# Five unread filler products taken out of a decode block's tail, and half of one row of small products cut narrower

## The chip, the core and the metric

The kernel runs on one core of one Trainium2 chip. TensorE (PE in the profile, its weight loads PEld), VectorE (DVE), ScalarE (ACT), GpSimd (POOL) and SyncE (SP, which issues most of the DMAs) each run their own list of instructions and wait for each other by semaphores. The metric is the time of one execution on the device in microseconds. TensorE's clock is granted by a throttle: the profile shows the granted share, 1.0 or 0.5.

## The reference

One decode step of a transformer block with conditioning, for two sequences (B = 2, one token each, D = 512), all in float32:

```python
mod = (silu(c) @ w_mod).reshape(2, 6, 1, 512)      # sa, ca, ga, sb, cb, gb
h = layernorm(x) * (1 + ca) + sa
x = x + ga * attention(h)                          # 32 query heads, 8 key heads of 128,
                                                   # last 4096 positions of the cache, then @ wo
h = layernorm(x) * (1 + cb) + sb
x = x + gb * (silu(h @ w1) @ w2)                   # w1: 512 x 1792, w2: 1792 x 512
```

The inputs that are read come to 97.5 MB, nearly all of it cache and weights, each read once.

## The kernel before

All weights and caches stream through a ring of eight slots in SBUF (`slots`), loaded by SP in the order of use: w_mod, wq, then keys and values in four groups each, wo, w1, w2. A load waits until the products that read its slots before are done.

TensorE's work is in program order (`inorder`). Products with a wide weight matrix keep two activation columns as the stationary operand in a 128x32 piece of the array, and stream 512 columns of weights past it; four such calls, one for each 32 columns of the array (g = 0 to 3), run side by side. In float32 a call stands as two products in the trace.

The tail of the kernel, to which the change belongs, is a chain:

1. `busy(4)` (L414): four filler products. `busy(n)` (L384) issues n products of `id4` with a zero tile `warm` of 512 columns into the PSUM bank `junk` (L382), which nobody reads.
2. wo: 32 calls into `acc_o` (L417).
3. `gather` (L396): ACT copies acc_o to SBUF in two halves (L400), and four calls of 128 columns add up the four pieces into `ao` (L404).
4. DVE turns ao, adds the residual to x1T and sums it (L433 to L444); TensorE forms the mean (L446), DVE the centred, scaled activations hT_b and the squares (L449 to L454).
5. w1: 16 calls of 448 columns into `hid` (L459), with the variance `var_b` between its halves (L468). ACT takes the root (L470).
6. DVE turns hid, scales it, and forms the SiLU with an exponential on ACT (L475 to L487); the result is uT.
7. w2: rows 0 to 10 as calls of 512 columns into `acc_yw` (L491). ACT copies that to `y_sb` in two halves (L513).
8. The last three rows of w2 are used the other way round, "turned" (L503): pieces of the weights are the stationary operand, 128x32 or, in the first of these rows, 128x64, and two columns of uT stream past. Between them the same form adds up y_sb. All go into `yx`.
9. DVE adds the residual (L524), and ACT issues the store (L525).

Five more fillers stand in the tail: one in `gather` behind ACT's copies (`fill=1`), one behind ao, one behind the mean and two behind w1's products.

The loads of w2 come in five pieces, rows 0 to 7, 8 to 10, 11, 12 and 13. The last four wait for slots that wo's products leave.

Of the kernel before, what the change touches and what calls it, by code (L numbers as in the profile page):

```python
# [23 lines left out]
def adaln_block(  # L24
# [34 lines left out]
    def const(shape, name):  # L59
        return consts.tile(shape, F32, name=name)  # L60

    def bank(tag, name):
        return (psum1 if tag in "CO" else psum).tile([P, 512], F32, tag=tag, name=name)
# [155 lines left out]
    hT, uT = const([P, 4, 32], "hT_b"), const([P, F // P, 32], "uT")  # L219
# [9 lines left out]
    for n in range(2):  # L229
        q_ps = bank("D", f"q{n}")  # L230
        for k in range(4):
            for g in range(4):
# [5 lines left out]
                    start=(k == 0),  # L238
                    stop=(k == 3),
# [3 lines left out]
        for g in range(G):  # L243
# [4 lines left out]
                start=True,  # L248
                stop=True,
# [134 lines left out]
    def busy(n):  # L384

        for _ in range(n):
            inorder(nc.tensor.matmul(  # L387
                junk[0:32, :],
                id4,
                warm,  # L390
                start=True,
                stop=True,
            ))


    def gather(acc, wide, name, start, stop, fill=0):  # L396

        sb_ = once.tile([P, D], F32, tag="wide", name=name)
        for c in (slice(0, D // 2), slice(D // 2, D)):
            inorder(nc.scalar.copy(sb_[:, c], wide[:, c]))  # L400
        if fill:
            busy(fill)
        for g in range(4):
            inorder(nc.tensor.matmul(  # L404
                acc[32 * g : 32 * g + 32, :],
                id4,
                sb_[:, g * P : (g + 1) * P],
                start=start,
                stop=stop,
            ))  # L410

    acc = bank("D", "acc_o")
    ao = bank("A", "ao")[:, :P]
    busy(4)  # L414
    for q in range(32):
# [5 lines left out]
            start=(q < 4),  # L421
            stop=(q >= 28),
        ))
    gather(ao, acc, "acc_o_sb", True, True, fill=1)
    busy(1)
    T2, WIDE = F // P, 11
    w2t = {}
    for lo, hi in ((0, 8), (8, 11), (11, 12), (12, 13), (13, T2)):
# [15 lines left out]
    nc.vector.tensor_reduce(ks, x1T.rearrange("p k b -> p b k"), axis=AX.X, op=ALU.add)  # L444
    mean = bank("B", "mean_b")
    inorder(nc.tensor.matmul(mean[:, :B], mean512, ks, start=True, stop=True))  # L446
    busy(1)
    dT = once.tile([P, 4, B], F32, tag="dT", name="dT")
    nc.vector.tensor_sub(dT, x1T, mean[:, None, :B].to_broadcast([P, 4, B]))  # L449
    nc.vector.tensor_mul(hT[:, :, 0:32:16], dT, cbT[:, :, 0:32:16])  # L450
# [6 lines left out]
    for k in range(4):  # L457
        for g in range(4):
# [4 lines left out]
                start=(k == 0),  # L463
                stop=(k == 3),
            ))
        if k == 1:
# [3 lines left out]
            nc.scalar.activation(std, var[:, :B], AF.Sqrt, bias=eps_t)  # L470
            rstd = once.tile([P, B], F32, tag="rstdb", name="rstd_b")
            nc.vector.reciprocal(rstd, std)
    busy(2)
    hidT = once.tile([P, T2, 32], F32, tag="pr", name="hidT")
    nc.vector.transpose(hidT, hp.rearrange("p (m t) -> p t m", t=T2))  # L475
    z = once.tile([P, T2, B], F32, tag="z", name="z")
# [12 lines left out]
    for tt in range(WIDE):  # L489
# [5 lines left out]
            start=(tt < 4),  # L495
            stop=(tt >= WIDE - 4),
        ))

    def turned_products(rows, u, ks=range(4), start=False, stop=False, m=32):

        for k in ks:
            for g in range(0, P, m):
                inorder(nc.tensor.matmul(  # L503
                    yT[g : g + m, k, :, 0],
                    rows[:, k * P + g : k * P + g + m],
                    u,
                    start=start and k == 0,
                    stop=stop and k == 3,
                ))
# [2 lines left out]
    for c in (slice(0, D // 2), slice(D // 2, D)):  # L512
        inorder(nc.scalar.copy(y_sb[:, c], yw[:, c]))  # L513
    for h, tt in enumerate(range(WIDE, T2)):
        turned_products(
            w2t[tt],
            uT[:, tt, 0:32:16],
            start=(h == 0),
            stop=(tt == T2 - 1),
            m=32 if h else 64,  # L520
        )
        if h < 2:
            turned_products(y_sb, id4[:, 0:32:16], range(2 * h, 2 * h + 2))
    inorder(nc.vector.tensor_tensor_scan(yo, g0, yx, 0.0, op0=ALU.mult, op1=ALU.add))  # L524
# [48 lines left out]
```

## Time and profile before

| | us |
|---|---|
| median of 3 runs | 233.94 (233.76 to 233.95) |
| the profiled execution | 233.89 |
| its span, first to last instruction | 232.3 |
| PE busy in the span | 125.5 (54%) |
| DVE, ACT, POOL busy | 21.9, 17.3, 5.2 |
| data moved | 97.66 MB, mean 420 GB/s |

The mean granted clock of TensorE over the span is 0.801. Times within the trace count from the start of the span. A row of the timeline or of a group gives the engine, the line of the kernel, the operation, `output<-inputs` by the program's names, shapes and a count; an arrow in brackets names what ended the idle time before it. `slots<-in_B_w_dram` stands for a load of w1 or w2. A stretch's row gives its length, the busy time and number of instructions of the engine asked for, the granted clock, the DMA share and the GB/s.

### The profile page before, as it was taken

What the parts mean: (1) busy time and instruction counts of PE and PEld (TensorE: products, weight loads), DVE (VectorE), ACT (ScalarE), POOL (GpSimd) and SP (SyncE); (2) the same over time, 40 slices, a digit from 0 to 9 for tenths busy, and PEclk for the clock granted to TensorE, in tenths of its full rate; (3) what the DMA queues carried; (4) which work ended last, traced back from release to release, by engine and by line L of the source; (5) the groups of instructions that cost most, each with busy time, mean ns of one, the idle gap of its engine ahead of it and who ended that gap; (6) DMA issues with size and microseconds to landing.
All of it is one profiled execution on the core that took longest, in us unless ns stands there. A gap on an engine that the chain in (4) does not pass through costs nothing.

```text
span 232.3 us, 2204 instructions
## 1 busy us (share of the span) xinstructions
PE 125.5 (54%) x976; PEld 42.4 (18%) x976; DVE 21.9 (9%) x74; ACT 17.3 (7%) x39; POOL 5.2 (2%) x22
## 2 busy tenths in 40 slices
PE   0004905840950781495096068139509506999877
PEld 0001401320210221121033012112202102232223
DVE  0005330110021000003000001200000210000230
ACT  2000210000012010001001000100100100000331
POOL 4003010000000000000000000000000000000000
PEclk9999995985796596578579659957857965999999
DMA  7999898998989989899899999999999999999993
GB/s 271 432 495 429 372 530 361 508 398 361 530 372 508 395 364 519 384 496 398 374 496 406 496 395 386 474 418 474 406 395 465 429 446 406 432 392 444 414 410 133
DMA packets 2916, 97.66 MB, mean 420 GB/s; under 512 B 460, under 2 KB 476, under 8 KB 1116
## 3 DMA queue, kind: packets, MB, share of 16 engines
q1 hardware_dynamic: 2748, 97.52, 97.6%
q8 instruction: 7, 0.11, 0.2%
q10 hardware_dynamic: 160, 0.01, 0.0%
q14 instruction: 1, 0.01, 0.0%
HBM read 97.53 MB, written 0.01 MB: 420 GB/s over the span
## 4 chain that ended last, share of the span: by engine, by line
DMA 76%; PE 22%; issue 1%; DVE 1%; SPq 0%
DMA slots<-in_A_v_cache_dram 50%; PE o L323 16%; DMA slots<-in_A_wq_dram 15%; DMA slots<-in_B_w_dram 10%; PE q L234 4%; PE acc_yw L491 1%; PE yx L503 1%; PE qT L244 0%; DVE q_sb L242 0%; SPq L102 0%; DVE xc L93 0%; DVE yo L524 0%
## 5 line engine op out<-in xcount | busy, mean ns | idle before, releaser
L272 PE MATMUL s<-slots,qs 128*32 128x512 f32 x256 | 36.6, 736 | 32.6 <-DMA slots<-in_A_k_cache_dram 32.6
L323 PE MATMUL o<-slots,probs 128*32 128x512 f32 x256 | 37.0, 739 | 25.5 <-DMA slots<-in_A_v_cache_dram 25.5
L323 PEld LDWEIGHTS o<-slots,probs 128*32 128x32 f32 x256 | 11.6, 129 | 47.7 <-issue 47.7
L272 PEld LDWEIGHTS s<-slots,qs 128*32 128x32 f32 x256 | 9.2, 132 | 56.7 <-issue 31.4
L197 PE MATMUL m_a<-slots,scT 128*32 128x256 f32 x32 | 4.0, 447 | 20.4 <-DVE scT L189 20.4
L234 PE MATMUL q<-slots,hq_T 128*32 128x512 f32 x64 | 8.9, 703 | 8.4 <-DMA slots<-in_A_wq_dram 8.4
L284 DVE TENSOR_REDUCE mx<-s 128x1 f32<-128x512 f32 x4 | 2.8, 692 | 68.1 <-PE s L272 68.1
L387 PE MATMUL junk<-warm,id 128*32 128x512 f32 x18 | 8.6, 595 | 0.3 <-DVE oTn L347 0.3
L336 ACT ACTIVATE ob<-o,rl 128x256 f32<-128x256 f32 x8 | 3.4, 470 | 64.7 <-PE o L323 64.7
L347 DVE COPY oTn<-oT 128x16 f32<-128x16 f32 x4 | 0.7, 185 | 67.9 <-PE oT L339 67.9
L417 PE MATMUL acc_o<-slots,oTn 128*32 128x512 f32 x64 | 7.1, 593 | 0.0
L200 PE MATMUL m_sp<-slots,scT 128*32 128x512 f32 x32 | 6.6, 712 | 0.0
L298 ACT COPY bias<-bp 128x1 f32<-128x1 f32 x4 | 0.6, 159 | 79.4 <-PE bp L294 79.4
L339 PE MATMUL oT<-id,ob 128*128 128x4 f32 x32 | 4.2, 255 | 2.3 <-ACT ob L336 2.3
L197 PEld LDWEIGHTS m_a<-slots,scT 128*32 128x32 f32 x32 | 1.1, 117 | 21.2 <-DVE scT L189 20.4
L339 PEld LDWEIGHTS oT<-id,ob 128*128 128x128 f32 x32 | 3.9, 191 | 5.9 <-ACT ob L336 5.9
L234 PEld LDWEIGHTS q<-slots,hq_T 128*32 128x32 f32 x64 | 2.3, 126 | 14.1 <-issue 14.1
L305 PE MATMUL lp<-rowsum,same 128*128 128x1 f32 x8 | 1.7, 282 | 5.6 <-ACT pr L300 3.2
L491 PE MATMUL acc_yw<-slots,uT 128*32 128x512 f32 x22 | 2.8, 599 | 1.6 <-DMA slots<-in_B_w_dram 1.6
L459 PE MATMUL hid<-slots,hT_b 128*32 128x448 f32 x32 | 3.4, 544 | 0.5 <-DMA slots<-in_B_w_dram 0.5
L303 DVE STREAM_TRANSPOSE probs<-pr 128x512 f32<-128x512 f32 x4 | 2.8, 711 | 7.2 <-ACT pr L300 7.2
L286 PE MATMUL mT<-ident,mx 128*1 128x128 f32 x8 | 1.5, 271 | 3.3 <-DVE mx L284 3.3
(108 smaller groups left out, 60.1 us busy)
## 6 DMA issues: line engine op xcount, KB each, us to landing
slots<-in_w_mod_dram SPq DMA_DIRECT2D x1, 6144.0 KB, 17.2
slots<-in_A_wo_dram SPq DMA_DIRECT2D x1, 6144.0 KB, 26.1
slots<-in_B_w_dram SPq DMA_DIRECT2D x1, 2688.0 KB
slots<-in_A_wo_dram SPq DMA_DIRECT2D x1, 2048.0 KB, 30.1
slots<-in_B_w_dram SPq DMA_DIRECT2D x1, 2048.0 KB
slots<-in_B_w_dram SPq DMA_DIRECT2D x1, 896.0 KB
slots<-in_B_w_dram SPq DMA_DIRECT2D x1, 768.0 KB
slots<-in_B_w_dram SPq DMA_DIRECT2D x3, 256.0 KB, 16.1
```

Of the source, the lines that this page charges most:

```text
L197: nc.tensor.matmul(m_a[r, :], scT[:, k, :], ab[:, g], start=(k == 0), stop=(k == 3))
L200: nc.tensor.matmul(m_sp[r, :], scT[:, k, :], cd[:, g], start=(k == 0), stop=(k == 3))
L234: inorder(nc.tensor.matmul(q_ps[32 * g : 32 * g + 32, :], hq_T[:, k, :], wqt[:, k, lo : lo + 4 * DH], start=(k == 0), stop=(k == 3),))
L272: inorder(nc.tensor.matmul(s_ps[32 * c : 32 * c + 32, :], stat(grp, v, s), kt[grp][:, lo : lo + 512], start=(s == 0 and v == 0), stop=(s = ...
L284: nc.vector.tensor_reduce(mx, s_ps, axis=AX.X, op=ALU.max)
L323: inorder(nc.tensor.matmul(o_ps[r : r + 32, :], probs[grp % 2][:, 32 * n + 16 * s : 32 * n + 16 * s + 32], vt[grp][:, lo : lo + 512], star ...
L336: nc.scalar.activation(o_sb[:, c], o_ps[:, c], AF.Copy, scale=rl)
L339: inorder(nc.tensor.matmul(cols[:, 4 * v : 4 * v + 4], o_sb[:, v * DH : (v + 1) * DH], id4[:, 4 * v : 4 * v + 4], start=True, stop=True,))
L387: inorder(nc.tensor.matmul(junk[0:32, :], id4, warm, start=True, stop=True,))
L417: inorder(nc.tensor.matmul(acc[32 * g : 32 * g + 32, :], oTn[:, q, :], wot[q], start=(q < 4), stop=(q >= 28),))
L459: inorder(nc.tensor.matmul(hp[32 * g : 32 * g + 32, :], hT[:, k, :], w1t[k][:, g * FC : (g + 1) * FC], start=(k == 0), stop=(k == 3),))
L491: inorder(nc.tensor.matmul(yw[32 * g : 32 * g + 32, :], uT[:, tt, :], w2t[tt], start=(tt < 4), stop=(tt >= WIDE - 4),))
```

## The change

Five calls of `busy` go: the one in `gather` with its parameter, and those behind ao, behind the mean and the two behind w1. The four ahead of wo's products stay. The first turned row of w2 (row 11) was eight calls of 128x64; now its first two groups of 128 outputs are eight calls of 128x32, and the other two are four of 128x64. What is added up is the same.

```diff
-    def gather(acc, wide, name, start, stop, fill=0):
+    def gather(acc, wide, name, start, stop):
 
         sb_ = once.tile([P, D], F32, tag="wide", name=name)
         for c in (slice(0, D // 2), slice(D // 2, D)):
             inorder(nc.scalar.copy(sb_[:, c], wide[:, c]))
-        if fill:
-            busy(fill)
         for g in range(4):
...
-    gather(ao, acc, "acc_o_sb", True, True, fill=1)
-    busy(1)
+    gather(ao, acc, "acc_o_sb", True, True)
...
     inorder(nc.tensor.matmul(mean[:, :B], mean512, ks, start=True, stop=True))
-    busy(1)
...
             nc.vector.reciprocal(rstd, std)
-    busy(2)
     hidT = once.tile([P, T2, 32], F32, tag="pr", name="hidT")
...
     for h, tt in enumerate(range(WIDE, T2)):
-        turned_products(
-            w2t[tt],
-            uT[:, tt, 0:32:16],
-            start=(h == 0),
-            stop=(tt == T2 - 1),
-            m=32 if h else 64,
-        )
+        for half in range(2):
+            turned_products(
+                w2t[tt],
+                uT[:, tt, 0:32:16],
+                range(2 * half, 2 * half + 2),
+                start=(h == 0),
+                stop=(tt == T2 - 1),
+                m=32 if h or half == 0 else 64,
+            )
```

TensorE's list from wo's products to w2's, before (a number behind a name is a buffer's):

```order
L417 MATMUL acc_o<-slots,oTn 32x512 x32
L387 MATMUL junk<-warm,id_58 32x512
L404 MATMUL ao<-acc_o_sb,id_58 32x128 x4
L387 MATMUL junk<-warm,id_58 32x512
L446 MATMUL mean_b<-ks,mean_101 128x2
L387 MATMUL junk<-warm,id_58 32x512
L459 MATMUL hid<-slots,hT_b 32x448 x8
L468 MATMUL var_b<-vs,mean_101 128x2
L459 MATMUL hid<-slots,hT_b 32x448 x8
L387 MATMUL junk<-warm,id_58 32x512 x2
L491 MATMUL acc_yw<-slots,uT 32x512 x11
```

And after:

```order
L415 MATMUL acc_o<-slots,oTn 32x512 x32
L402 MATMUL ao<-acc_o_sb,id_58 32x128 x4
L443 MATMUL mean_b<-ks,mean_101 128x2
L455 MATMUL hid<-slots,hT_b 32x448 x8
L464 MATMUL var_b<-vs,mean_101 128x2
L455 MATMUL hid<-slots,hT_b 32x448 x8
L486 MATMUL acc_yw<-slots,uT 32x512 x11
```

Only the fillers are gone; the order of the rest stays. The end of the same list, the turned products, after:

```order
L498 MATMUL yx<-uT,slots 32x2 x8
L498 MATMUL yx<-uT,slots 64x2 x4
L498 MATMUL yx<-id_58,y_sb 32x2 x8
L498 MATMUL yx<-uT,slots 32x2 x16
L498 MATMUL yx<-id_58,y_sb 32x2 x8
L498 MATMUL yx<-uT,slots 32x2 x16
```

Before, one row of eight calls of 64x2 stood in place of the first two rows here.

## The prediction

> **What bounds the kernel now.** I read the page first, for the share of each resource and the chain that ended last.
>
> ```profile
> span 232.3 us, 2204 instructions
> PEclk9999995985796596578579659957857965999999
> DMA  7999898998989989899899999999999999999993
> DMA 76%; PE 22%; issue 1%; DVE 1%; SPq 0%
> ```
>
> The loads are busy almost to the end, and three quarters of the chain is loads. The granted clock of the tensor engine goes up and down all through the kernel, and only the last six slices stand at full speed together. All edits lie in those slices, so I read the timeline of TensorE from the last products of wo to the first of w1.
>
> ```profile
> 214.11 1.04 PE L417 MATMUL acc_o<-slots,oTn 128*32 128x512 f32 x8
> 214.96 1.02 PE L387 MATMUL junk<-warm,id 128*32 128x512 f32 x2
> 215.70 0.57 PE L404 MATMUL ao<-acc_o_sb,id 128*32 128x128 f32 x6
> 216.04 0.59 PE L387 MATMUL junk<-warm,id 128*32 128x512 f32 x1
> 216.10 0.28 PE L404 MATMUL ao<-acc_o_sb,id 128*32 128x128 f32 x2
> 216.47 0.59 PE L387 MATMUL junk<-warm,id 128*32 128x512 f32 x1
> 217.41 0.38 PE L446 MATMUL mean_b<-ks,mean 128*128 128x2 f32 x2 [0.35 <-DVE ks L444]
> 217.72 1.04 PE L387 MATMUL junk<-warm,id 128*32 128x512 f32 x2
> 219.25 1.71 PE L459 MATMUL hid<-slots,hT_b 128*32 128x448 f32 x16 [0.48 <-DMA slots<-in_B_w_dram]
> ```
>
> Each call stands as two products in the trace. The hid products start when w1 lands, not when TensorE is free. The whole timeline has the rest of the tail.
>
> ```profile
> 209.18 5.44 SPq L86 DMA_DIRECT2D slots<-in_B_w_dram  x4
> 217.19 0.16 DVE L444 TENSOR_REDUCE ks<-x1T 128x2 f32<-128x8 f32 x1
> 220.89 0.38 PE L468 MATMUL var_b<-vs,mean 128*128 128x2 f32 x2
> 221.21 1.71 PE L459 MATMUL hid<-slots,hT_b 128*32 128x448 f32 x16
> 222.73 1.88 PE L387 MATMUL junk<-warm,id 128*32 128x512 f32 x4
> 225.16 0.21 DVE L487 TENSOR_TENSOR uT<-z,sgh 128x28 f32<-128x28 f32 x1
> 226.25 2.81 PE L491 MATMUL acc_yw<-slots,uT 128*32 128x512 f32 x22 [1.64 <-DMA slots<-in_B_w_dram]
> 228.99 0.63 PE L503 MATMUL yx<-uT,slots 128*64 128x2 f32 x16
> 229.18 0.65 ACT L513 COPY y_sb<-acc_yw 128x256 f32<-128x256 f32 x2 [4.63 <-PE acc_yw L491]
> 229.60 0.31 PE L503 MATMUL yx<-id,y_sb 128*32 128x2 f32 x16
> ```
>
> The path to the end is: w2 lands, acc_yw, ACT's copy, the small yx products. The activation uT is done at 225.16 + 0.21 = 225.37 and could release acc_yw some 0.06 us later (mean_b began at 217.41, ks ended at 217.35), while the load holds acc_yw until 226.25. So the way through hid has 226.25 - 225.43 = 0.82 us of slack. That is all that covers it.
>
> **The clock, read from stretches.** The granted clock changes at 88.46, 166.97 and 231.82 us, between rows shown here; these points are 23 and 19 steps of 3.413 us apart, and every row below lies inside one step of that grid and shows one clock. I asked for the busy time of the wide products (512 columns) step by step, attention's o first. The columns are the stretch, its length, busy and count, clock, DMA share, GB/s. What a step held shows in the clock of the next row.
>
> ```profile
> 85.05:88.45 3.40, 1.31 (x13) 1.00 0.98 424
> 88.46:91.86 3.40, 0.00 (x0) 0.50 0.76 328
> 163.56:166.95 3.39, 0.97 (x12) 1.00 0.80 348
> 166.97:170.36 3.39, 0.00 (x0) 0.50 1.16 503
> 201.11:204.50 3.39, 1.62 (x16) 1.00 1.07 464
> 204.52:207.91 3.39, 0.00 (x0) 1.00 0.77 329
> ```
>
> The same for the score products s, and for all products in the last two steps:
>
> ```profile
> 143.08:146.47 3.39, 1.45 (x16) 1.00 0.98 425
> 146.49:149.89 3.40, 0.00 (x0) 1.00 0.84 366
> 95.29:98.69 3.40, 2.39 (x12) 0.50 0.80 347
> 98.71:102.10 3.39, 3.39 (x20) 0.50 1.25 541
> 102.12:105.51 3.39, 3.39 (x36) 1.00 0.89 387
> ```
>
> ```profile
> 228.42:231.81 3.39, 2.16 (x118) 1.00 0.13 42
> 231.83:232.30 0.47, 0.00 (x0) 0.50 0.06 5
> ```
>
> At full clock a step with 1.45 us of wide products held it, and one with 1.31 us lost it. At half clock 2.39 us of 3.40 did not bring it back and a full step did. Small products count for little: the step of 85.05 also had the row below, and the step of 228.42 was 2.16 us busy, most of it with yx, and still fell.
>
> ```profile
> L339 PE MATMUL oT<-id,ob 128*128 128x4 f32 x8 | 1.1, 256 | 0.6 <-ACT ob L336 0.6
> ```
>
>  I take 1.4 us as the least that holds and between 2.4 and 3.3 us as what restores, the middle being 2.6 (estimates from these rows). The last two rows also price half clock: of the 20 and 36 products four each had begun in the step before, so 16 and 32 start in 3.41 us, 0.85 and 0.43 us for a group of four.
>
> **The change part by part.** Five calls of 128x512 go, ten products in the rows of 214.96, 216.04, 216.47, 217.72 and 222.73. None of them is on the path at full clock: the next work behind each waits for ACT, DVE or a load. The direct saving is 0; its bounds are 0 and 0.03 us (the last pair of ao may come a little sooner), and that is covered by w1's landing.
>
> What they did is fill the steps of the clock. Without them TensorE has, between the end of acc_o (214.11 + 1.04 = 215.15) and hid at 219.25, eight products of 128 columns and two of two columns. In the profiled grid the step 214.76 to 218.16 then holds 0.39 of acc_o, 0.68 of ao and 0.38 of mean_b, 1.45 us busy of any kind, of which 0.39 is wide. That is under 1.31, so **the clock falls at 218.17**, before hid. A window of 3.41 us fits into the nearly bare 4.1 us wherever the grid lies, but for some 0.15 us of its positions.
>
> For the profiled grid the sum goes on so:
> - hid at full clock: groups of four at 1.71 less a tail of 0.21, over four, 0.375 us; at half 0.75. The first half ends at 219.25 + 4 x 0.75 = 222.25. The piece with var_b costs 221.21 - 220.75 = 0.46 at full, 0.46 to 0.92 at half; I take 0.70, since it is mostly latency: 222.95.
> - The step 218.17 to 221.58 holds 2.33 us of hid, less than the 2.39 that did not lift. So half clock lasts to 224.99: 2.04/0.75 = 2.7 groups; the other 1.3 take 0.49 and the tail 0.21. hid ends at 225.69, before at 221.21 + 1.71 = 222.92: 2.77 us late.
> - uT shifts as much, to 228.14, and acc_yw starts at 228.20, 1.95 late (2.77 less the slack).
> - The step 224.99 to 228.40 has 0.7 of hid and 0.2 of acc_yw: **the clock falls a second time**, at 228.41. The six groups of acc_yw: half of one before, four in the full step at half clock, 1.5 x 0.43 after it. The last group's end is 232.46, before it was 226.25 + 2.81 - 0.17 = 228.89: **3.57 us late**.
> - What follows (copy, yx, the store) is as before.
>
> The profiled execution took 233.89 us, 1.59 around its span of 232.3, and lies 0.05 under the median of 233.94. With this grid the result is 233.89 + 3.6 = 237.5.
>
> No run here shows whether the grid starts with the program. So I did the same sum with it shifted. With the fall at 220.2, hid runs at full until then, is lifted at 223.6 and ends at 224.47; acc_yw starts at 226.97, falls at 227.0, and ends 2.4 late: 236.3. With the fall at 219.07 the next step is nearly full of hid (219.25 to 222.48), the clock is back at 222.48, hid ends 1.5 late and acc_yw starts 0.6 late but at full clock: 234.5. The cases part where the step behind the fall just holds enough of hid to lift (fall at 218.3: 218.3 + 3.41 - 219.25 = 2.46 us), and where the step after the lift just holds 1.4 us of acc_yw (fall at about 219.5). So, as estimates: falls from 217.4 to 218.3, 27% of the 3.41 us of positions, give 3.2 to 3.6 us; from 218.3 to 219.5, a good third, 0.4 to 0.7; later ones, 38%, 2.1 to 2.4.
>
> The page "TensorE: Matmul & The Clock Gate" of the Trainium skill, section "What's actually happening", calls the window of 3413 ns free-running, not reset when a kernel starts; the grid above agrees with the length, and no run here shows the rest. By it executions would scatter over all positions, with a median near 236.2.
>
> **The first turned row.** Eight calls of 128x64 (16 products in 0.63) become eight of 128x32 and four of 128x64. By the row of 229.60, 16 narrow products take 0.31; half of the wide ones take 0.3. Both ends of the row lie in ACT's copy: its first half is done at 229.18 + 0.33 = 229.51 at the soonest, and the y_sb products start at 229.60. I put it at 0, bounds -0.1 (the narrow ones begin sooner behind acc_yw) and +0.2 (all of it at half clock, 1.2 instead of 0.6, no longer under the copy). SP's queue is not touched: its last loads wait for acc_o, and no product goes before that.
>
> **The rivals.**
>
> One fall only. hid is slowed, and the clock is back before acc_yw: 0.4 to 0.7 us, 234.3 to 234.6. For it speak a third of the grid positions, against it the profiled grid.
>
> The clock holds. If a step loses it only when it has no product at all, nothing falls: the longest bare stretches would be 217.79 to 219.25 and 222.92 to 226.25, 3.33 us, and no grid step of 3.41 fits. Then the time is 233.9. Against it stand the steps of 85.05 and 163.56, with 13 and 12 wide products each, that fell.
>
> "TensorE: Matmul & The Clock Gate" of the Trainium skill, in the same section, lets the gate close "after ≥1 idle window (~3.4µs)". Taken by the letter that is this rival; the two rows disagree.
>
> Faster, by loads. If the fillers' reads slow the DMA, w2 lands sooner without them.
>
> ```profile
> 211.35:214.74 3.39, 3.39 (x36) 1.00 1.06 451
> 214.76:218.16 3.40, 3.05 (x19) 1.00 0.95 407
> 221.59:224.98 3.39, 3.02 (x20) 1.00 0.97 414
> ```
>
> These are the steps of all TensorE work without fillers and with them: 40 GB/s less with fillers. Over 6.8 us that is 0.27 MB, or 0.6 us of loading, and acc_yw could start at 225.65: 233.3. It decides only if the clock holds too, and if uT is not over 0.3 us late: beyond that less than the 0.47 us named below is left. Against it: the step at 88.46 moved 328 GB/s with no product at all, so the swing is the loads' own.
>
> **How the numbers follow.** Two falls get 0.57 (two thirds of the positions, by 0.85 that the step rule holds), one fall 0.28, the clock holds 0.10, faster by loads 0.05. The likeliest is two falls: 236.0 to 237.6, and **236.5 us** as its time, between the larger group at 236.2 and the profiled grid at 237.5. The range for eight in ten takes in one fall, and at the top the dearer var_b and yx: **234.2 to 237.8**. A measurement of this kernel tells 0.2%, 0.47 us, from no change. Slower: two falls and three quarters of one fall, 0.78; same: the holding clock and the rest, 0.17; faster: 0.05.
>
> **What would show it.** The granted clock in the step after acc_o: 0.5 from a point between 217.4 and 220.7. hid products of some 950 ns each in the groups by line, where the first row below stands now (the second row, from the step of 95.29, has s at half clock, 512 columns).
>
> ```profile
> L459 PE MATMUL hid<-slots,hT_b 128*32 128x448 f32 x32 | 3.4, 544 | 0.5 <-DMA slots<-in_B_w_dram 0.5
> L272 PE MATMUL s<-slots,qs 128*32 128x512 f32 x12 | 2.8, 1061 | 8.3 <-DMA slots<-in_A_k_cache_dram 8.3
> ```
>
> Further, acc_yw released by DVE's uT and no longer by a load. If the clock is 1.0 through hid, the step rule is wrong, and with it the forecast; if hid is slow and acc_yw is not, the rival of one fall is right; if the loads end before 229 us, the last one is.

## The result and the profile after

The changed kernel took 236.74 us in the median of 6 executions (234.65 to 237.68), the kernel before 233.87 beside it (233.76 to 234.09). The ratio over these executions is 1.011, 95% interval 1.0066 to 1.0155. **It is 1.1% slower, and its executions scatter over 3 us where those of before agree within 0.33.** The profiled execution took 237.68 us, at the upper end. Two executions of the experiments below, of 266.82 and 636.18 us, lie far outside all others and are in none of their figures.

The page of the profiled execution, to be held against the first fence of the prediction:

```profile
span 236.1 us, 2200 instructions
PEclk9999985985795595587589569759659957999577
DMA  7998999989898999989898999999898999899960
DMA 72%; PE 24%; DVE 1%; issue 1%; SPq 0%; ACT 0%; ACTq 0%
```

The row of the clock ended in 999999 and now ends in 999577. The loads are done a slice earlier in the row, because the row is longer. Their share of the chain fell, TensorE's rose. The steps of the clock's grid in the tail (stretch, length, TensorE's busy time and count, clock, DMA share, GB/s):

```profile
215.08:218.48 3.40, 1.28 (x14) 1.00 0.97 411
218.50:221.89 3.39, 2.42 (x16) 0.50 1.05 447
221.91:225.30 3.39, 3.39 (x21) 0.50 0.96 410
225.32:228.72 3.40, 0.91 (x12) 1.00 0.83 331
228.74:232.13 3.39, 3.39 (x21) 0.50 0.09 31
232.15:235.54 3.39, 2.12 (x124) 1.00 0.00 0
```

The step behind wo's products is 1.28 us busy, and the next step runs at half clock. That one, with 2.42 us of hid, does not bring the clock back; the full one after it does. Then the near empty step between hid and acc_yw loses the clock again, and acc_yw runs at half. TensorE's timeline says the same in products:

```profile
215.86 0.69 PE L402 MATMUL ao<-acc_o_sb,id 128*32 128x128 f32 x8 [0.57 <-ACT acc_o_sb L400]
217.57 0.38 PE L443 MATMUL mean_b<-ks,mean 128*128 128x2 f32 x2 [1.03 <-DVE ks L441]
219.47 3.21 PE L455 MATMUL hid<-slots,hT_b 128*32 128x448 f32 x16 [1.51 <-DMA slots<-in_B_w_dram]
222.61 0.59 PE L464 MATMUL var_b<-vs,mean 128*128 128x2 f32 x2
223.12 2.77 PE L455 MATMUL hid<-slots,hT_b 128*32 128x448 f32 x16
228.39 4.04 PE L486 MATMUL acc_yw<-slots,uT 128*32 128x512 f32 x19 [2.50 <-DVE uT L482]
232.25 0.61 PE L486 MATMUL acc_yw<-slots,uT 128*32 128x512 f32 x3
```

The first 16 hid products took 3.21 us where they took 1.71. acc_yw is now released by DVE's uT, no longer by a load, and ends at 232.86 instead of 229.06.

### The profile page after: what moved, and what is told of

The parts are those of the page before. It is cut to its first block, busy times and chain, and to the rows that moved or that the text cites. A ratio compares the mean times of both kernels' runs of the same rounds, so it can differ in the third digit from the quotient of the medians.

```text
span 236.1 us, 2200 instructions
## 1 busy us (share of the span) xinstructions
PE 126.5 (54%) x974; PEld 44.3 (19%) x974; DVE 21.9 (9%) x74; ACT 17.3 (7%) x39; POOL 5.2 (2%) x22
## 4 chain that ended last, share of the span: by engine, by line
DMA 72%; PE 24%; DVE 1%; issue 1%; SPq 0%; ACT 0%; ACTq 0%
DMA slots<-in_A_v_cache_dram 49%; PE o L323 15%; DMA slots<-in_A_wq_dram 15%; DMA slots<-in_B_w_dram 8%; PE q L234 4%; PE hid L455 3%; PE acc_yw L486 2%; PE yx L498 0%; PE qT L244 0%; DVE q_sb L242 0%; SPq L102 0%; DVE hidT L470 0%; PE var_b L464 0%; DVE z L473 0%; ACT y_sb L508 0%
## 5 line engine op out<-in xcount | busy, mean ns | idle before, releaser
L455 PE MATMUL hid<-slots,hT_b 128*32 128x448 f32 x32 | 6.0, 891 | 1.5 <-DMA slots<-in_B_w_dram 1.5
L486 PE MATMUL acc_yw<-slots,uT 128*32 128x512 f32 x22 | 4.5, 924 | 2.5 <-DVE uT L482 2.5
L415 PEld LDWEIGHTS acc_o<-slots,oTn 128*32 128x32 f32 x64 | 3.5, 110 | 3.3 <-issue 3.0
L387 PE MATMUL junk<-warm,id 128*32 128x512 f32 x8 | 3.6, 595 | 0.3 <-DVE oTn L347 0.3
```

The lines of the kernel that those rows point to most:

```text
L387: inorder(nc.tensor.matmul(junk[0:32, :], id4, warm, start=True, stop=True,))
L415: inorder(nc.tensor.matmul(acc[32 * g : 32 * g + 32, :], oTn[:, q, :], wot[q], start=(q < 4), stop=(q >= 28),))
L455: inorder(nc.tensor.matmul(hp[32 * g : 32 * g + 32, :], hT[:, k, :], w1t[k][:, g * FC : (g + 1) * FC], start=(k == 0), stop=(k == 3),))
L486: inorder(nc.tensor.matmul(yw[32 * g : 32 * g + 32, :], uT[:, tt, :], w2t[tt], start=(tt < 4), stop=(tt >= WIDE - 4),))
```

## The experiments

The theory: a step of the clock's grid that streams too few columns loses the full clock; the fillers did nothing but stream. The rivals: a product of any kind keeps the clock; the fillers' number counts, not their place; the row of narrow pieces has a part in it.

### The fillers behind wo's products alone

```diff
-    busy(2)
     hidT = once.tile([P, T2, 32], F32, tag="pr", name="hidT")
```

> The kernel before without the two fillers behind w1's products; the three behind wo's stay. Step theory (a 3.41 us step of the clock's grid that holds under about 1.4 us of wide products loses the full clock): hid runs at full clock in every execution, uT is done near 225.4 us as before, and the bare 3.5 us between hid and acc_yw (222.7 to 226.25) loses the clock before or within acc_yw for most grid positions. Over all positions: 0 to 2.7 us longer than before, in the middle +1.6, executions scattered. Rival, only a step with no product at all loses it: no change, all executions within 0.3 us of each other.

Measured: 235.6 us in the middle of five executions, ratio 1.0091 (1.0061 to 1.0122), from 235.38 to 237.6. The middle, +1.7, is as expected; the longest, +3.7, lies above the expected 2.7, and there is no trace of it. Two of the steps of the traced one (236.56), and its hid and acc_yw:

```profile
221.63:225.02 3.39, 1.34 (x16) 1.00 0.96 410
225.04:228.44 3.40, 2.08 (x12) 0.50 0.87 347
```

```profile
221.26 1.71 PE L459 MATMUL hid<-slots,hT_b 128*32 128x448 f32 x16
226.36 5.34 PE L490 MATMUL acc_yw<-slots,uT 128*32 128x512 f32 x22 [3.39 <-DMA slots<-in_B_w_dram]
```

hid is as before and acc_yw starts with its load as before, but it takes 5.34 us instead of 2.81. This is the second fall by itself. The rival that asks for a wholly empty step is out: this step had 16 products.

### The fillers behind w1's products alone

```diff
-    gather(ao, acc, "acc_o_sb", True, True, fill=1)
-    busy(1)
+    gather(ao, acc, "acc_o_sb", True, True)
...
     inorder(nc.tensor.matmul(mean[:, :B], mean512, ks, start=True, stop=True))
-    busy(1)
```

> The kernel before without the three fillers behind wo's products; the two behind w1's stay. Step theory: the clock falls between 217.4 and 220.7 us, hid runs partly or wholly at half clock (some 950 ns a product) and ends 1.3 to 2.8 us late; the two fillers behind it fill the step ahead of acc_yw, so that acc_yw is late by hid's delay less 0.8 us of slack and runs at full clock. Over all positions +0.4 to +2.0 us, middle +0.7. The sum of this and of the run without w1's fillers need not be the change's. Rival, the wait of w1's load hides hid: no change.

Measured: 235.14 us, ratio 1.0052 (1.0035 to 1.0070), from 234.3 to 235.72, inside the expected span; the middle, +1.3, is higher than the expected +0.7.

```profile
216.67:220.07 3.40, 1.59 (x18) 1.00 0.93 396
220.09:223.48 3.39, 3.39 (x21) 0.50 1.00 429
223.50:226.89 3.39, 3.01 (x20) 1.00 0.96 403
```

```profile
227.30 2.77 PE L489 MATMUL acc_yw<-slots,uT 128*32 128x512 f32 x22 [0.80 <-DVE uT L485]
```

The first fall by itself: hid is slow, acc_yw starts late, but at full clock, since the fillers behind hid fill the step before it.

### The fillers made thin

The five fillers stay as instructions, with 32 columns in place of 512; the four ahead of wo stay wide.

```diff
-    def busy(n):
+    def busy(n, cols=512):
...
-                junk[0:32, :],
+                junk[0:32, :cols],
-                warm,
+                warm[:, :cols],
```

> The kernel before with the five fillers kept as instructions, but 32 columns wide instead of 512 (the four ahead of wo stay at 512). Step theory, which counts streamed columns and not instructions: 5 x 2 x 0.027 us are too little, so it goes as with no fillers: clock falls ahead of hid, +0.4 to +3.7 us over the positions, middle +2.2. Rival, any product in a step keeps the clock: as before, +0.

Measured: 234.58 us, ratio 1.0063 (1.0034 to 1.0092), 12 executions from 234.08 to 237.27: seven up to 234.7, five from 235.38 to 237.27. The traced one took 236.09:

```profile
216.57:219.97 3.40, 1.43 (x16) 1.00 0.97 409
219.99:223.38 3.39, 3.39 (x22) 0.50 1.00 427
223.40:226.79 3.39, 1.07 (x16) 1.00 0.95 393
226.81:230.21 3.40, 3.36 (x16) 0.50 0.48 182
```

Both falls are there. Ten filler products were issued where they were before, and the steps of 216.57 and 223.40, with 16 products each, lost the clock all the same: columns count, not products. The median is 0.7 us above before, under the expected +2.2 and the changed kernel's; the span of times is much the same, and the runs do not say how much of the lower median is chance.

### The changed kernel again, at other positions of the grid

Nothing is edited in these three.

> The changed kernel once more, for more executions and another position of the clock's grid. Step theory with a grid that does not start with the program: executions scatter in groups at 234.3 to 234.6, 236.0 to 236.3 and 237.1 to 237.6, and the traced one follows the sum for the position that its own trace shows: a fall before 218.3 to 218.5 gives 3.2 to 3.7, from there to 219.5 it gives 0.4 to 0.8, later ones 2.1 to 2.4. Rival, a grid bound to the program: the time of the first trace, 237.5, in nearly all.

> The changed kernel, one look for one more position of the clock's grid. The trace's own fall ahead of hid sets the time: a fall before 218.3 to 218.5 us gives +3.2 to +3.7 over 233.9, from there to 219.5 one fall and +0.4 to +0.8, later +2.1 to +2.4 (times of falls as if w1 lands at 219.2; its landing shifts them by a few tenths). Rival, the time does not follow the position.

> The same, one look more: if its fall lies in another of the three stretches than the traces before, its time lies in that stretch's group.

The first: 235.84 us, 11 executions from 234.28 to 237.52; its traced one took 237.02, the kernel before 233.82 beside it.

```profile
214.09:217.48 3.39, 1.82 (x21) 1.00 0.96 410
217.50:220.89 3.39, 1.91 (x14) 0.50 1.04 441
220.91:224.31 3.40, 3.40 (x22) 0.50 0.95 408
224.33:227.72 3.39, 0.89 (x14) 1.00 0.98 399
227.74:231.13 3.39, 3.39 (x17) 0.50 0.21 79
```

A fall at 217.49, which belongs to the group of 3.2 to 3.7; measured +3.2. The second took 234.68:

```profile
216.22:219.61 3.39, 1.34 (x14) 1.00 0.97 409
219.63:223.03 3.40, 3.40 (x22) 0.50 1.05 451
223.05:226.44 3.39, 1.54 (x16) 1.00 0.94 393
226.46:229.85 3.39, 2.77 (x38) 1.00 0.62 240
```

One fall at 219.62, and none before acc_yw. It lies 0.1 us beyond the border of 219.5, as near as the expectation allows for the landing of w1, and belongs to the group of one fall by its time. The third took 233.73, with 234.19 for the one run of before beside it:

```profile
214.07:217.46 3.39, 1.83 (x22) 1.00 0.94 404
217.48:220.88 3.40, 1.92 (x19) 1.00 1.03 437
220.90:224.29 3.39, 1.89 (x18) 1.00 0.93 397
224.31:227.70 3.39, 1.59 (x16) 1.00 0.99 403
227.72:231.11 3.39, 2.60 (x130) 1.00 0.21 78
```

**With none of the five fillers this execution kept its clock to the end of the products and lost no time.** Its first step differs from the one of 214.09 by 0.02 us of grid. So, as far as this one execution shows, the fillers' absence costs only by the clock.

All 19 executions of the changed kernel: 233.73; seven from 234.28 to 234.78; four from 235.37 to 236.27; seven from 237.02 to 237.68. Median 235.84. The four traces have their first fall at 218.49, 217.49, 219.62 and nowhere, and their times are 237.68, 237.02, 234.68 and 233.73. None of the four lies in the middle group, 235.37 to 236.27; the trace with thin fillers does (236.09), with falls at 219.98 and 226.80. The grid does not start with the program.

### One filler less

```diff
-    gather(ao, acc, "acc_o_sb", True, True, fill=1)
+    gather(ao, acc, "acc_o_sb", True, True)
```

> The kernel before without the one filler inside the gather; the other four stay. Step theory: the longest stretch that this bares, 214.98 to 216.2 with 0.4 us of ao in it, is too short to put any grid step of 3.41 us under 1.4 us of wide products, so the clock holds everywhere: 233.9 within 0.2 us and no scatter. Rival, every filler counts: part of the loss, +0.3 us or more.

Measured: 233.86 us, ratio 0.9999 (0.9990 to 1.0008), from 233.63 to 234.13. It is not the number of fillers that counts: this version is as fast as the kernel before, with one call less.

### The row alone

The kernel before with the second edit alone.

```diff
-            m=32 if h else 64,
+                range(2 * half, 2 * half + 2),
...
+                m=32 if h or half == 0 else 64,
```

> The kernel before with the second edit alone: half of the first turned row in 128x32 pieces, all fillers kept. Theory: 0, within 0.1 us, since both ends of the row lie under ACT's copy of acc_yw; the narrow pieces begin up to 0.1 us sooner behind acc_yw, and the y_sb products still begin 0.05 us behind the first half of the copy. Rival, the switch to 64-wide pieces now stands right ahead of the y_sb products and delays them: +0.1 to +0.2 us.

Measured: 235.55 us, ratio 1.0062 (1.0044 to 1.0079); ten of 12 executions from 235.29 to 236.0, two at 233.8. Both expectations missed. Its chain of waits, the last rows:

```profile
229.56 0.96 PE yx L503 x74
230.52 1.73 issue
232.25 0.21 PE yx L503
232.46 0.02 issue
232.48 0.19 DVE yo L526
```

and the timeline:

```profile
230.12 0.41 PE L503 MATMUL yx<-uT,slots 128*32 128x2 f32 x29
232.25 0.19 PE L503 MATMUL yx<-uT,slots 128*32 128x2 f32 x1 [1.73 <-issue]
```

Everything up to 230.5 is on time. Then TensorE stands still without waiting for anything that the profile shows, and a single product comes 1.7 us later. The DMA packets of the trace have seven of 16,384 bytes on the queue of instructions, the last of them from 229.55 to 230.85. So I supposed that the last product lay in a block of TensorE's list that was fetched too late: the narrower row adds 16 instructions (eight more products, each with its weight load). The packet alone does not show it: the kernel before has the same seven, the last from 229.67 to 230.65, and no late product, and here the product starts 1.4 us after the packet has ended, which no trace explains. The Trainium skill, page "Runtime: NRT & Kernel Launch", section "Terms", has the engines' instruction memory refilled in 16 KiB blocks; the packets, of 16,384 bytes each, agree with that size.

### Sixteen instructions elsewhere

The old row; behind w1's two fillers, four thin ones.

```diff
     busy(2)
+    busy(4, 32)
```

> The kernel before with its first turned row as it was, and four more filler calls of only 32 columns behind w1's two: 16 more instructions on TensorE, as many as the narrower row adds, in a place where TensorE is idle. Theory, the last instructions of TensorE's list come in a block that is fetched too late once the list is over its border: +1.6 to +1.8 us in most executions, with the last turned product issued at about 232.2 us and TensorE idle before it for 1.7 us with nothing waited for. Rival, the narrow pieces or the switch of the piece's width cost that time: no change, 233.9.

Measured: 235.07 us, ratio 1.0035 (1.0015 to 1.0056), ten executions in two groups: four from 233.72 to 234.08, six from 235.06 to 235.91.

```profile
229.09 1.50 PE yx L504 x90
230.59 1.44 issue
232.03 0.21 PE yx L504
```

The same single late product without the row: **the length of the list costs the time, not the row.** It does so in most executions, not in all, and the traces say nothing of why. That a block of the list is fetched too late stays an inference from the list's length and the packets.

### The row with room

The row, with the filler in the gather gone (12 instructions more than before) and then with another one ahead of wo gone (8 more).

```diff
-    gather(ao, acc, "acc_o_sb", True, True, fill=1)
+    gather(ao, acc, "acc_o_sb", True, True)
```

> The kernel before with the narrower row, and without the one filler inside the gather, so that TensorE's list has 12 instructions more than before instead of 16. By the last run's trace the border lay two instructions ahead of the end, so this list ends two short of it. Theory of the block: no stall, 233.9 within 0.2 us. Rival, the row itself costs 1.7 us: 235.5.

```diff
-    busy(4)
+    busy(3)
```

> The narrower row with more room: the kernel before without the filler inside the gather and with three instead of four ahead of wo's products, so that TensorE's list is 8 instructions longer than before, where the run with 12 had two groups of executions, at 233.7 to 234.0 and at 234.2 to 234.6. Theory, the row itself costs nothing and the second group came from the end rows of TensorE's list, which lay over the border of the last block: 233.85 within 0.15 us, at most a few executions above 234.2. Rival, the row costs 0.3 us by itself: 234.1 as with 12.

And the old row with 12 instructions more:

> The old row, the kernel before without the filler inside the gather and with four fillers of 32 columns behind w1's two: 12 instructions more than before, none of them in the row. Theory of the block: the same two groups as the narrower row with 12 more, 233.7 to 234.0 and 234.2 to 234.6, median about 234.1. Rival, the row costs 0.3 us: no second group, 233.85.

With 12 more and the row: 234.11 us, ratio 1.0013 (1.0003 to 1.0023), five executions from 233.74 to 234.0, five from 234.22 to 234.59. With 12 more and the old row: 234.1, ratio 1.0013 (1.0004 to 1.0022), six from 233.84 to 234.1, four from 234.33 to 234.6. With 8 more and the row: 233.9, ratio 1.0002 (0.9993 to 1.0011), no second group. The row itself costs nothing. The first of the three expectations, 233.9 within 0.2, was narrowly missed with 234.11; its rival, 235.5, is out, and the other two expectations held. With 12 more no product is late in either trace. The small rest is at the program's end. SP's waits have it, with 12 more and the row, with 12 more and the old row, and before:

```profile
SPq L569 <- PEq L569: 1.3, 2, 0.7
```

```profile
SPq L568 <- PEq L568: 1.4, 2, 0.8
```

```profile
SPq L567 <- PEq L567: 1.0, 2, 0.6
```

SP waits longer for TensorE's own last steps, which are the end of its list. From the end of the last product to the end of the execution it is 3.62 and 3.70 us with 12 more, 3.31 before and 3.30 with 8 more. The traced execution with 3.62 took 234.0 us and counts to the lower group, because its w2 landed 0.2 us sooner than before; so the two groups of times do not part the executions with a late end from those without.

## Why the prediction was right

The range held, the direction too, and the time was 0.24 us off in the first six executions (0.66 above the median of all 19). That closeness is in part luck: with executions scattered over 3 us, the median of six hangs on which positions of the grid came up. The mechanism is what the runs bear out.

**Fillers off the path, cover for the clock.** Right. Three of the four traced executions lose the clock where the sum puts it. The fourth, with its grid at 217.47 just inside the positions from 217.4 on that the sum lets fall, kept it and lost nothing. One filler less cost nothing.

**The sum for the profiled grid.** By luck its position came up nearly unchanged in the first trace, 0.3 us later, so that the two can be held against each other. The piece with var_b, from the end of hid's fourth group (219.47 + 4 x 0.75 = 222.47) to 223.12: 0.65, put at 0.70. hid's end 225.89, put at 225.69; w1 had landed 0.2 later in this execution. The start of acc_yw 228.39, put at 228.20. Its last group's end 232.25 + 0.61 - 0.17 = 232.69, put at 232.46. The total is 3.8, put at 3.6; the same sum with this trace's own landing (219.47) and grid (218.49) gives 232.73 - 228.89 = 3.84.

**The grid's positions.** The groups came out at 0.4 to 0.9, 1.5 to 2.4 and 3.2 to 3.8, where 0.4 to 0.7, 2.1 to 2.4 and 3.2 to 3.6 were forecast. The step of the working that was mis-sized is "I take 1.4 us as the least that holds". Two steps that began at 214.08 and 214.06 lost the clock and kept it. In the timelines, the last rows of acc_o, first in the one that lost it, then in the one that kept it:

```profile
213.48 1.50 PE L415 MATMUL acc_o<-slots,oTn 128*32 128x512 f32 x12
```

```profile
207.93 7.07 PE L415 MATMUL acc_o<-slots,oTn 128*32 128x512 f32 x64
```

Less the tail of 0.17, in which nothing streams any more, they end at 214.81 and 214.83, and both steps have 0.43 us of ao (four passes of 128 columns, a quarter of 0.43 each). That is 1.16 and 1.20 us of streaming, so the least that holds is about 1.2.

All the traces together say it more sharply. Take each product for its columns from its start on, 0.43 us for 512 at full clock and twice that at half, and count what runs side by side once; these two steps then come to 1.20 and 1.25. The fourteen traces have 463 whole steps at full clock. The 144 that lost it hold up to 1.22 us, the 319 that kept it 1.23 or more. At half clock, the 252 steps that stayed there hold up to 2.57 us, and the 135 that brought the clock back 2.61 or more. So the 2.6 for restoring was right, and the 1.4 for holding was read from busy times with tails in them.

The lower border widens the group of one fall and the positions without a fall, at the cost of "later ones, 38%, 2.1 to 2.4": by their times these are 4 of 19. Two falls came to 11 of 19, put at 0.57; one fall to 7, put at 0.28.

**Hidden loads' rival.** With the clock held and no fillers, acc_yw was still released by its load, at 226.11 in the last trace:

```profile
226.11 2.81 PE L486 MATMUL acc_yw<-slots,uT 128*32 128x512 f32 x22 [3.32 <-DMA slots<-in_B_w_dram]
```

Before it was 226.25. That is within the scatter of the loads (226.36 in the run with three fillers and no others). The 0.6 us of this rival are not there.

**The clock holds.** Right to be small: a step with 14 or 16 products falls. The one execution of 19 that kept its clock did so by its position, not because only an empty step would lose it. The Trainium skill, "TensorE: Matmul & The Clock Gate", section "What's actually happening", asks for a whole idle window; these steps were not idle, so the rule is too mild for this kernel. The free-running window of the same section is borne out by the four positions.

**The first turned row.** Put at 0, and 0 it is in the changed kernel. But the part "I put it at 0, bounds -0.1 ... and +0.2" priced the products and never the list they stand in: alone, the edit costs 1.7 us. In the changed kernel the fillers' 20 instructions pay for the row's 16, so the list is 4 shorter than before.

## What to carry to other kernels

Look at the clock step by step before you take out work that nobody reads: off the path it may be what keeps the path at full clock, and its price is the slowdown of everything up to the next step that is full enough to bring the clock back. When times scatter in groups, find what free-running thing the groups belong to, and predict the groups rather than one number. Count instructions as well as time when you split products at the very end of a list.

## What the runs showed of the hardware that I had not expected

- The clock's edge is sharp: at full clock every step with at most 1.22 us of streaming in 3.41 lost it and every step with 1.23 or more kept it, and at half clock the border lies between 2.57 and 2.61 (463 and 387 steps). Two executions of the same kernel, whose steps differ by 0.02 us of grid, kept and lost the clock there, and ended 3.3 us apart (233.73 and 237.02).
- Products of four columns or two count next to nothing: the step of 228.42 before was 2.16 us busy, most of it with yx, and fell. A filler that uses a quarter of the array's width holds the clock nevertheless: in the trace of the row alone, the step from 222.90 to 226.31 was 1.70 us busy, 1.62 of it with fillers, and kept it.
- With 16 instructions more in TensorE's list, the last product came 1.4 and 1.7 us late in the two traces, and ten of 12 and six of ten executions are longer by 1.2 to 2.1 us. With 8 more nothing of it showed in 11 executions. With 12 more the end of the program came 0.3 and 0.4 us late in the two traces. That the cause is a block of the list that is fetched too late is inferred.
